# Low parts of weights and tokens moved from GpSimd to VectorE, PSUM banks split 3 and 5, and a new order of the MLPs' work

## The chip, the cores and the metric

The kernel runs on one core of a Trainium2 chip. The metric is device time in microseconds (us) of one execution, the median of three runs. One execution was also taken with the hardware profiler; all rows below are from that one.

## The reference

Attention with a threshold, then two MLPs on its output of 2304 tokens of 512 features. Everything is float32.

```python
def _attn_ref(q, k, v, tau):                      # 4 x 8 heads, 576 x 64
    scores = scale * np.matmul(q, k.transpose(0, 1, 3, 2))
    thresh = np.max(scores, axis=-1, keepdims=True) - tau
    scores = np.where(scores >= thresh, scores, -1000000000.0)
    ...
    return np.matmul(attn, v)
def _moe_ref(x, w_in, w_out):                     # 512 x 2048, 2048 x 512
    h = x @ w_in
    return (h * np.tanh(softplus(h))) @ w_out
def _moe2_ref(x, w_gate, w_val, w_out):           # 512 x 1536 twice, 1536 x 512
    g = x @ w_gate
    silu = g * (1.0 / (1.0 + np.exp(-g)))
    return (silu * (x @ w_val)) @ w_out
```

## The kernel before

Every product of the MLPs is three TensorE products: each operand is split into a high part, which ScalarE rounds, and a low part, the operand less its high part. The weights come as 64-bit words; VectorE and GpSimd take them apart and round them, and then split them.

The work is a list of steps. For each, the program gives an engine, an estimated cost, what must be done before, which buffers it takes and frees, and a rank. A planner (`Plan.run`) plays the list through with those costs: at each moment, among the steps whose estimated start lies within 0.06 us of the earliest, it takes the one with the lowest rank. What results is a fixed order of instructions on each engine. On the chip each engine works through its queue in that order, and an instruction that waits holds up all behind it.

The MLPs are cut into 140 units, numbered t from 0: 80 of the first MLP, 60 of the second. A unit is one block of 128 hidden features for one chunk of tokens; there are five chunks, four of 512 tokens and one of 256. The weights' blocks are worked off in groups (of 2, 2, 3, 3, 4, 2 blocks, then of 2, 3, 3, 2, 2); in a group, for each chunk, its blocks follow each other and add up in the same four PSUM banks, and then the sums leave PSUM. Unit numbers of the first groups: 0 to 9, 10 to 19, 20 to 34. The steps are called:

- U, of 12 matmuls: products with the first weights (`project`). In the second MLP U is the gate and a second one of 12 the value (called U2 in the code, V here with its unit, as V106). Each takes one bank of the pool `h`.
- E: Mish or Silu on ScalarE, which frees the bank of U. times: gate by value on VectorE, which frees the bank of V.
- H and O: the high part on ScalarE (line 541), the low part on VectorE (line 544).
- D0 to D139, of 12 matmuls: products with the last weights (`down`), in four quarters d, each into its own bank of the pool `y`. D of a unit needs its O.
- S: the eviction of a finished sum, four for a chunk, named by the last unit of the group on that chunk (S1,0 to S1,3 for chunk 0 of the first group). In an MLP's first group ScalarE copies it (line 572), later VectorE adds it to what is in SBUF (line 574). S frees its bank of `y`; D of the next chunk waits for that.
- w4 to w67: the weight tiles that are made beside the MLPs (w0 to w3 are made beside attention). For each: a load, then a, b (VectorE), u (GpSimd, line 443), c, d, e, x (VectorE; the last is line 457), h (ScalarE, line 462), and the low part (line 467, GpSimd).
- x and X, x2 and X2: high and low part of the tokens that an MLP reads, four pieces for each chunk (lines 548 and 551, ScalarE and GpSimd). The X of chunks 1 to 4 come at the start of the first MLP, the X2 of all five chunks at the change from the first to the second MLP.

The numbers of buffers and the ranks are in these lines (677 and 679):

```python
MSLOTS = dict(h=4, y=4, t=3, g=3, wraw=2, wc=2, wt=11)
MRANK = dict(X=-12.5, w=-17, U=1.5, U2=-13, D=21.5, E=-45, V=-28.5, H=-20, O=-17.5, S=19.5, x2=26.5, out=-40)
```

Of the kernel before, what the change touches and what calls it, by code (L numbers as in the profile page):

```python
# [20 lines left out]
def f(ap):  # L21
    return ap.bitcast(F32)
# [388 lines left out]
class Weights:  # L411
# [7 lines left out]

    def ops(self, plan, k, rank, place, t1, f1, t2, f2, after=()):  # L420

# [42 lines left out]
        def lo():  # L464
            m, j, _ = self.tiles[k]
            t = self.done[id(m), j]
            nc.gpsimd.tensor_tensor(out=t[:, 1], in0=f(self.n[k]), in1=f(t[:, 0]), op=ALU.subtract)  # L467

        K = lambda s: ("w", k, s)
        for eng, cost, fn, s, deps, take, free in (  # L470
            ("DMA", 1.46, load, "l", "", t1, []),
            ("DVE", .335, a, "a", "l", t2, []),
            ("DVE", .602, b, "b", "a", [], []),
            ("Pool", 1.0, up, "u", "b", [], []),
            ("DVE", .335, c, "c", "a", [], []),
            ("DVE", .335, d, "d", "u", [], []),
            ("DVE", .602, e, "e", "d", [], f1),
            ("DVE", .602, x, "x", "ec", [], []),
            ("ACT", .52, hi, "h", "x", [("wt", k)], []),
            ("Pool", 1.225, lo, "", "h", [], f2),  # L480
        ):
            plan.op(eng, cost, fn, K(s), [K(y) for y in deps] + list(after) * (s == "h"), take, free, rank - (20 if s == "l" else 0))


def moes(tc, cp, acc, W, uses, x0, units1, units2, w_in, w_out, w_gate, w_val, w_out2, out, chunk):
# [125 lines left out]
    for k in range(len(W.tiles)):  # L611
        if k < NEARLY:
            plan.given.add(("w", k, ""))
        else:
            W.ops(plan, k, when[uses[k]] + MRANK["w"], place, ["wraw"], ["wraw"], ["wc"], ["wc"])
    prev = {}
    for t, un in enumerate(units1 + units2):
# [33 lines left out]
        for d in range(width):  # L651
# [4 lines left out]
            if un["one"]:  # L656
# [131 lines left out]
```

## Time and profile before

| | us |
|---|---|
| median of three runs (lowest, highest) | 1183.14 (1181.34, 1183.83) |
| the profiled execution | 1182.31 |
| its span, first to last instruction | 1180.5 |
| TensorE busy in the span | 1125.4 |
| VectorE busy | 778.0 |
| ScalarE busy | 457.5 |
| GpSimd busy | 352.2 |

In the rows PE is TensorE, PEld its weight loads, DVE VectorE, ACT ScalarE, POOL GpSimd. Times in rows count from the span's start. Attention takes the first 314 us, the MLPs the rest. The 1.8 us between span and execution lie around the program.

### The profile page before, as it was taken

To read this page: it belongs to the slowest core of one execution; us is meant where nothing else is said; L and a number is where in the kernel's file an instruction comes from. 1 tells how busy PE (TensorE), PEld (TensorE's weight loads), DVE (VectorE), ACT (ScalarE), POOL (GpSimd) and SP (SyncE) were. 2 spreads that over 40 slices of the span, in tenths; PEclk is the share of its full clock that TensorE was granted. 3 is DMA by queue.
4 is the path that set the end of the run, shared out by engine and by line. 5 is a ranking of instruction groups with operands and counts; after the bars stand their busy time and mean duration, and the time that the engine had idled before them with its cause. 6 is when DMAs were issued, how large, how long until landed. Compare 5 with 4: busy or idle time off the path is not lost.

```text
span 1180.5 us, 16366 instructions
## 1 busy us (share of the span) xinstructions
PE 1125.4 (95%) x6088; PEld 928.3 (79%) x6088; DVE 778.0 (66%) x1291; ACT 457.5 (39%) x897; POOL 352.2 (30%) x452
## 2 busy tenths in 40 slices
PE   1899999999997999999999998999999999999998
PEld 1687777777686888888888876888888788888887
DVE  7888887888489883593753599627525873586333
ACT  3788787787644322232222233333111221121111
POOL 4555444443475330130210256502101320141000
PEclk9999999999999999999999999999999999999999
DMA  6465665664013211110120122101101120120012
GB/s 191 102 163 155 153 172 144 153 164 129 12 56 102 76 37 36 36 57 16 37 72 1 36 57 70 53 1 46 62 1 37 54 72 1 36 72 1 1 72 90
DMA packets 34272, 83.25 MB, mean 71 GB/s; under 512 B 5264, under 2 KB 5264, under 8 KB 34192
## 3 DMA queue, kind: packets, MB, share of 16 engines
q1 hardware_dynamic: 34192, 82.20, 24.6%
q8 instruction: 48, 0.79, 0.3%
q14 instruction: 32, 0.26, 0.1%
HBM read 50.92 MB, written 4.72 MB: 47 GB/s over the span
## 4 chain that ended last, share of the span: by engine, by line
PE 81%; DVE 11%; POOL 2%; DMA 2%; issue 2%; SPq 1%; ACT 1%; ACTq 0%; DVEq 0%; POOLq 0%
PE h L524 24%; PE y L535 13%; PE y L537 12%; PE v L524 12%; PE s L89 7%; PE av L172 6%; PE tg L149 6%; POOL xlo L551 2%; DVE gl L544 1%; DVE cg L453 1%; DVE cg L436 1%; DVE cn L457 1%; DVE cn L446 1%; DVE cg L439 1%; DVE cg L449 1%
## 5 line engine op out<-in xcount | busy, mean ns | idle before, releaser
L544 DVE TENSOR_TENSOR gl<-s,gh 128x512 fp32r<-128x512 f32 (+1 forms) x140 | 104.6, 748 | 122.9 <-ACT gh L541 122.8
L541 ACT CAST gh<-s 128x512 fp32r<-128x512 f32 (+1 forms) x140 | 81.0, 579 | 253.8 <-DVE s L565 111.4
L524 PE MATMUL h<-xhi,wt 128*128 128x512 f32 (+1 forms) x576 | 170.7, 363 | 0.0
L467 POOL TENSOR_TENSOR wt<-cn,wt 128x512 fp32r<-128x512 f32 x42 | 59.4, 1418 | 321.2 <-ACT wt L462 276.6
L89 PE MATMUL s<-stk 128*128 128x320 f32 (+5 forms) x672 | 126.0, 317 | 26.6 <-DVE pp L126 14.7
L565 DVE TENSOR_TENSOR s<-v,u 128x512 f32<-128x512 f32 (+1 forms) x60 | 38.1, 635 | 170.6 <-PE v L524 170.6
L535 PE MATMUL y<-gh,wt 128*128 128x512 f32 (+1 forms) x400 | 115.0, 372 | 10.8 <-DVE acc L574 9.2
L89 PEld LDWEIGHTS s<-stk 128*128 128x128 f32 (+1 forms) x672 | 98.1, 190 | 34.0 <-issue 19.9
L108 DVE TENSOR_REDUCE sm<-s 128x1 f32<-128x576 f32 x144 | 108.7, 755 | 24.0 <-PE s L89 23.8
L126 DVE SCALAR_TENSOR_TENSOR pp<-s,sm,e 128x576 f32<-128x576 f32 x144 | 116.0, 806 | 4.6 <-POOL sm L112 1.1
L524 PEld LDWEIGHTS h<-xhi,wt 128*128 128x128 f32 x576 | 104.8, 189 | 17.0
L118 ACT ACTIVATE e<-s,sm 128x576 f32<-128x576 f32 x144 | 109.3, 759 | 8.9 <-DVE sm L108 8.1
L149 PE MATMUL tg<-idf,pp 128*128 128x128 f32 x656 | 104.0, 284 | 3.6 <-DVE pp L126 2.3
L524 PE MATMUL h<-xlo,wt 128*128 128x512 f32 (+1 forms) x288 | 104.7, 363 | 0.0
L443 POOL TENSOR_TENSOR cg<-cg,ione 128x512 int32<-128x512 int32 x68 | 82.3, 1211 | 72.8 <-DVE cg L439 69.3
L155 ACT COPY pt<-tg 128x384 f32<-128x384 f32 x192 | 87.2, 493 | 32.1 <-PE tg L149 31.8
L524 PE MATMUL h<-xhi,early 128*128 128x512 f32 (+1 forms) x320 | 94.4, 362 | 0.0
L535 PEld LDWEIGHTS y<-gh,wt 128*128 128x128 f32 x400 | 73.2, 191 | 25.0 <-issue 8.4
L556 ACT ACTIVATE s<-h 128x512 f32<-128x512 f32 (+1 forms) x80 | 44.3, 555 | 121.6 <-PE h L524 117.9
L149 PEld LDWEIGHTS tg<-idf,pp 128*128 128x128 f32 x656 | 72.7, 142 | 23.6 <-ACT pt L155 5.0
L562 ACT ACTIVATE u<-h 128x512 f32<-128x512 f32 (+1 forms) x60 | 33.2, 554 | 141.1 <-PE h L524 141.1
L467 POOL TENSOR_TENSOR early<-cn,early 128x512 fp32r<-128x512 f32 x26 | 36.9, 1420 | 164.2 <-ACT early L462 129.8
(108 smaller groups left out, 2337.1 us busy)
## 6 DMA issues: line engine op xcount, KB each, us to landing
raw<-in_dram SPq DMA_DIRECT2D x64, 512.0 KB, 3.5
stk<-kh SPq DMA_DIRECT2D x60, 144.0 KB, 2.7
stk<-kl SPq DMA_DIRECT2D x60, 144.0 KB, 2.6
vn<-in_dram SPq DMA_DIRECT2D x16, 320.0 KB, 2.9
out_dram<-acc SPq DMA_DIRECT2D x18, 256.0 KB, 2.1
qn<-in_dram SPq DMA_DIRECT2D x15, 288.0 KB, 3.2
kn<-in_dram SPq DMA_DIRECT2D x15, 288.0 KB, 3.7
stk<-qh SPq DMA_DIRECT2D x30, 144.0 KB, 3.8
```

The costliest lines, as they stand in the source:

```text
L89: nc.tensor.matmul(out=s[out, c0:c0 + n], lhsT=stk[:, 0, qc:qc + out.stop - out.start], rhs=stk[:, w, kc:kc + n], start=w == 1, stop=w == 2)
L108: nc.vector.tensor_reduce(out=d["nm"][:, i:i + 1], in_=d["s", i], op=ALU.max, axis=AX.X, negate=True)
L118: nc.scalar.activation(out=e, in_=d["s", i], func=AF.Exp, bias=d["nm"][:, i:i + 1])
L126: nc.vector.scalar_tensor_tensor(out=d["pp", c][:, 576 * h:576 * h + 576], in0=d["s", i], scalar=d["th"][:, i:i + 1], in1=d["e", i], op0=A ...
L149: nc.tensor.transpose(g[:, 128 * m:128 * m + 128], d["pp", c][:, o:o + 128], idf)
L155: nc.scalar.copy(out=t[:, m0:m0 + n, 128 * (c % 2):128 * (c % 2) + 128], in_=g[:, 0:n])
L443: nc.gpsimd.tensor_tensor(out=g, in0=g, in1=self.ione.to_broadcast([P, 512]), op=ALU.add)
L467: nc.gpsimd.tensor_tensor(out=t[:, 1], in0=f(self.n[k]), in1=f(t[:, 0]), op=ALU.subtract)
L524: nc.tensor.matmul(out=un[nm], lhsT=w[:, a, P * d:P * d + P], rhs=parts(x, d, un["c0"], un["n"]), start=d == 0 and k == 0, stop=d == ND - ...
L535: nc.tensor.matmul(out=y[:, 0:un["n"]], lhsT=w[:, a, P * d:P * d + P], rhs=x, start=first and k == 0, stop=last and k == 2)
L537: nc.tensor.matmul(out=y, lhsT=x[:, P * d:P * d + P], rhs=w[:, a], start=first and k == 0, stop=last and k == 2)
L544: V.tensor_tensor(out=un["gl"], in0=un["s"], in1=f(un["gh"]), op=ALU.subtract)
```

## The change

Four things change, all in the MLPs.

1. The low part of the weights w4 to w67 (line 467 before) goes from GpSimd to VectorE. Those of w0 to w3, beside attention, stay on GpSimd.
2. The low part of the second MLP's tokens (X2) goes from GpSimd to VectorE. That of the first MLP's (X) stays.
3. `h` has three banks and `y` five.
4. The ranks are new, and each step of a weight has a rank of its own, where one rank served all ten. The planner's costs of some steps change too (GpSimd's steps and matmuls a little dearer).

```diff
-            nc.gpsimd.tensor_tensor(out=t[:, 1], in0=f(self.n[k]), in1=f(t[:, 0]), op=ALU.subtract)
+            (V if low == "DVE" else nc.gpsimd).tensor_tensor(out=t[:, 1], in0=f(self.n[k]), in1=f(t[:, 0]), op=ALU.subtract)
...
-            ("Pool", 1.225, lo, "", "h", [], f2),
+            (low, .602 if low == "DVE" else 1.4, lo, "", "h", [], f2),
...
-            plan.op(eng, cost, fn, K(s), [K(y) for y in deps] + list(after) * (s == "h"), take, free, rank - (20 if s == "l" else 0))
+            plan.op(eng, cost, fn, K(s), [K(y) for y in deps], take, free, rank[s])
...
-                    plan.op("Pool", po(n), lambda a=(d, c0, un["n"]): x_lo(*a), ("X2", c0, d), [("x2", c0, d)], [], [], r + MRANK["x2"])
+                    plan.op("DVE", dv(n), lambda a=(d, c0, un["n"]): x_lo(*a, V), ("X2", c0, d), [("x2", c0, d)], [], [], r + MRANK["x2"])
...
-MSLOTS = dict(h=4, y=4, t=3, g=3, wraw=2, wc=2, wt=11)
-
-MRANK = dict(X=-12.5, w=-17, U=1.5, U2=-13, D=21.5, E=-45, V=-28.5, H=-20, O=-17.5, S=19.5, x2=26.5, out=-40)
+MSLOTS = dict(h=3, y=5, t=3, g=3, wraw=2, wc=2, wt=11)
+
+MRANK = dict(X=319.9, wl=-583.5, ..., wh=2429.7, w=589.2, U=-76.1, U2=-833.8, D=-58.3, E=1768.7, V=-350.2, H=-1017.8, O=572.6, S=-939.1, x2=686.6, out=-1641.3)
...
-            W.ops(plan, n, EARLY[n], place, ["wraw"], ["wraw"], ["wc"], ["wc"])
+            W.ops(plan, n, {x: EARLY[n] - 20 * (x == "l") for x in ("l", "a", "b", "u", "c", "d", "e", "x", "h", "")}, place, ["wraw"], ["wraw"], ["wc"], ["wc"], "Pool")
```

TensorE's order in attention is the same as before; on GpSimd two neighbours there change places. The order of the MLPs is new throughout. Three places follow.

**The start of the MLPs.** VectorE's queue before, from the last piece of attention's output on (`acc` is that output, `cg` and `cn` a weight in the making, `gl` the result of O):

```order
L210 TENSOR_TENSOR acc_61<-av15_1_4111,rs15_1_4122 128x320
L436 TENSOR_SCALAR cg_4172<-raw_4171 128x512
L544 TENSOR_TENSOR gl_4201<-s_4190,gh_4200 128x512
L439 SCALAR_TENSOR_TENSOR cg_4172<-raw_4171,cg_4172 128x512
L446 TENSOR_SCALAR cn_4173<-raw_4171 128x512
L436 TENSOR_SCALAR cg_4187<-raw_4186 128x512
L439 SCALAR_TENSOR_TENSOR cg_4187<-raw_4186,cg_4187 128x512
L544 TENSOR_TENSOR gl_4229<-s_4216,gh_4228 128x512
```

The same place now, from the first step of a weight on:

```order
L437 TENSOR_SCALAR cg_4169<-raw_4168 128x512
L440 SCALAR_TENSOR_TENSOR cg_4169<-raw_4168,cg_4169 128x512
L447 TENSOR_SCALAR cn_4170<-raw_4168 128x512
L437 TENSOR_SCALAR cg_4187<-raw_4186 128x512
L440 SCALAR_TENSOR_TENSOR cg_4187<-raw_4186,cg_4187 128x512
L447 TENSOR_SCALAR cn_4188<-raw_4186 128x512
L450 TENSOR_SCALAR cg_4169<-cg_4169 128x512
L454 SCALAR_TENSOR_TENSOR cg_4169<-raw_4168,cg_4169 128x512
L450 TENSOR_SCALAR cg_4187<-cg_4187 128x512
L458 SCALAR_TENSOR_TENSOR cn_4170<-cn_4170,cg_4169 128x512
L454 SCALAR_TENSOR_TENSOR cg_4187<-raw_4186,cg_4187 128x512
L545 TENSOR_TENSOR gl_4243<-s_4229,gh_4242 128x512
```

O0 stood behind one step of a weight; now it stands behind eleven, five of them behind two steps u of GpSimd. GpSimd's queue has u of w4 and w5 after the first five X now, where they stood after all sixteen. On ScalarE, the queue at the same place, before (`xhi` is x, `s` the result of E, `gh` that of H):

```order
L548 CAST xhi_4153<-acc_61 128x512 x6
L556 ACT_TABLE_LOAD
L556 ACTIVATE s_4190<-h_4158 128x512
L548 CAST xhi_4153<-acc_61 128x512
L541 CAST gh_4200<-s_4190 128x512
L548 CAST xhi_4153<-acc_61 128x512 x2
L556 ACTIVATE s_4216<-h_4181 128x512
```

and now:

```order
L549 CAST xhi_4153<-acc_61 128x512 x12
L549 CAST xhi_4153<-acc_61 128x256 x4
L557 ACT_TABLE_LOAD
L557 ACTIVATE s_4229<-h_4158 128x512
L557 ACTIVATE s_4234<-h_4182 128x512
L542 CAST gh_4242<-s_4229 128x512
L542 CAST gh_4249<-s_4234 128x512
```

E0 stood after six of the sixteen x; now it stands after all of them.

**The first evictions of the second pair of chunks (S3), on ScalarE.** Before (`acc<-y` is S, `wt` the high part of a weight):

```order
L541 CAST gh_4386<-s_4352 128x512
L556 ACTIVATE s_4406<-h_4380 128x512
L572 COPY acc_61<-y_4347 128x512
L572 COPY acc_61<-y_4359 128x512
L572 COPY acc_61<-y_4366 128x512
L541 CAST gh_4431<-s_4406 128x512
L572 COPY acc_61<-y_4375 128x512
```

and now:

```order
L557 ACTIVATE s_4393<-h_4353 128x512
L463 CAST wt7_4396<-cn_4281 128x512
L542 CAST gh_4420<-s_4393 128x512
L557 ACTIVATE s_4445<-h_4415 128x512
L463 CAST wt8_4451<-cn_4360 128x512
L573 COPY acc_61<-y_4388 128x512
L573 COPY acc_61<-y_4398 128x512
L573 COPY acc_61<-y_4404 128x512
L542 CAST gh_4474<-s_4445 128x512
```

S3,0 stood behind E6; now the high part of w8 is between. Further down before, the high part of w8 stood between two pieces of S5.

**The end of the first MLP, on TensorE** (each `y` is one bank; `y_7499` and `y_7507` are the first of D78, the next chunk's sum, `h` is U). Before:

```order
L535 MATMUL y_7422<-gh_7303,wt31_6809 128x512 x2
L535 MATMUL y_7422<-gl_7304,wt31_6809 128x512
L535 MATMUL y_7427<-gh_7303,wt31_6809 128x512 x2
L535 MATMUL y_7427<-gl_7304,wt31_6809 128x512
L535 MATMUL y_7499<-gh_7364,wt30_6389 128x256 x2
L535 MATMUL y_7499<-gl_7365,wt30_6389 128x256
L535 MATMUL y_7507<-gh_7364,wt30_6389 128x256 x2
L535 MATMUL y_7507<-gl_7365,wt30_6389 128x256
```

and now:

```order
L536 MATMUL y_7423<-gh_7305,wt31_6805 128x512 x2
L536 MATMUL y_7423<-gl_7306,wt31_6805 128x512
L536 MATMUL y_7433<-gh_7305,wt31_6805 128x512 x2
L536 MATMUL y_7433<-gl_7306,wt31_6805 128x512
L525 MATMUL h_7464<-x0h_85,early2_83 128x512
L525 MATMUL h_7464<-x0l_86,early2_83 128x512
L525 MATMUL h_7464<-x0h_85,early2_83 128x512 x2
L525 MATMUL h_7464<-x0l_86,early2_83 128x512
```

D78 followed D77 at once; now U81 and V81, 24 matmuls, stand between. Where D35 and D50 open a new sum, a whole U stands ahead of each now; before, it was none and a quarter of one.

## Rows read from the trace of the kernel before

**Rows 1.** The page's first part: busy time and share of the span of each engine.

```profile
PE 1125.4 (95%) x6088; PEld 928.3 (79%) x6088; DVE 778.0 (66%) x1291; ACT 457.5 (39%) x897; POOL 352.2 (30%) x452
```

**Rows 2.** Stretches: length, each engine's busy us (instructions), granted clock, DMA.

```profile
core 0: us, PE busy (x) PEld busy (x) DVE busy (x) ACT busy (x) POOL busy (x), PEclk, DMA share, GB/s
355.00:400.00 45.00, 38.37 (x169) 30.89 (x168) 44.51 (x60) 17.62 (x37) 23.40 (x17) 0.96 0.28 89
...
700.00:745.00 45.00, 37.34 (x173) 31.19 (x172) 41.07 (x51) 16.63 (x30) 28.89 (x22) 0.92 0.20 59
...
679.00:742.00 63.00, 55.34 (x260) 46.34 (x259) 59.88 (x78) 23.66 (x43) 39.47 (x29) 0.95 0.23 67
```

**Rows 3.** Waits of TensorE: who for whom, us in total, times, longest.

```profile
PE y L535 <- DVE acc L574: 10.0, 4, 6.0
PE y L535 <- ACT acc L572: 6.6, 4, 3.2
...
PE y L537 <- ACT gh L541: 0.9, 1, 0.9
```

**Rows 4.** Timeline of TensorE at the two longest waits: start, us, [idle before].

```profile
363.19 1.22 PE L535 MATMUL y<-gh,early 128*128 128x512 f32 x2 [3.15 <-ACT acc L572]
...
364.63 1.05 PE L535 MATMUL y<-gh,early 128*128 128x512 f32 x2
...
738.16 0.77 PE L535 MATMUL y<-gh,wt 128*128 128x256 f32 x2 [5.99 <-DVE acc L574]
```

**Rows 5.** The chain that ended last: start, us, what; one undisturbed U.

```profile
403.95 2.72 PE h L524 x12
```

**Rows 6.** Timeline of ScalarE at the wait of 363 us.

```profile
362.03 0.62 ACT L462 CAST wt<-cn 128x512 fp32r<-128x512 f32 x1 [4.96 <-DVE cn L457]
362.56 0.58 ACT L572 COPY acc<-y 128x512 f32<-128x512 f32 x1
```

**Rows 7.** Timeline of VectorE, four steps of weights between 346 and 365 us.

```profile
346.09 0.42 DVE L446 TENSOR_SCALAR cn<-raw 128x512 int32<-128x512 int32 x1
...
360.14 1.26 DVE L446 TENSOR_SCALAR cn<-raw 128x512 int32<-128x512 int32 x1
361.32 0.68 DVE L457 SCALAR_TENSOR_TENSOR cn<-cn,cg 128x512 f32<-128x512 f32 x1
...
363.10 1.65 DVE L457 SCALAR_TENSOR_TENSOR cn<-cn,cg 128x512 f32<-128x512 f32 x1
```

**Rows 8.** Timeline of GpSimd at the same time.

```profile
359.69 1.42 POOL L443 TENSOR_TENSOR cg<-cg,ione 128x512 int32<-128x512 int32 x1 [1.90 <-DVE cg L439]
362.73 1.46 POOL L467 TENSOR_TENSOR wt<-cn,wt 128x512 fp32r<-128x512 f32 x1 [1.61 <-ACT wt L462]
```

**Rows 9.** Groups by line and shape, whole span: count, busy us, mean ns.

```profile
L443 POOL TENSOR_TENSOR cg<-cg,ione 128x512 int32<-128x512 int32 x68 | 82.3, 1211 | 72.8 <-DVE cg L439 69.3 <-PE y L535 2.4 <-PE y L537 1.1
...
L467 POOL TENSOR_TENSOR wt<-cn,wt 128x512 fp32r<-128x512 f32 x42 | 59.4, 1418 | 321.2 <-ACT wt L462 276.6 <-DVE cg L439 42.2 <-issue 2.1
```

**Rows 10.** Timeline at the start of the MLPs, TensorE, ScalarE, GpSimd, then VectorE.

```profile
314.68 0.50 PE L524 MATMUL h<-x0h,early 128*128 128x512 f32 x1 [0.67 <-DVE acc L210]
...
314.70 3.23 ACT L548 CAST xhi<-acc 128x512 fp32r<-128x512 f32 x6 [3.07 <-DVE acc L210]
317.94 1.28 ACT L556 ACT_TABLE_LOAD   x1
...
325.67 1.02 ACT L548 CAST xhi<-acc 128x256 fp32r<-128x256 f32 x3
...
315.40 21.59 POOL L551 TENSOR_TENSOR xlo<-acc,xhi 128x512 fp32r<-128x512 f32 x16 [8.21 <-ACT xhi L548]
...
320.90 1.37 DVE L544 TENSOR_TENSOR gl<-s,gh 128x512 fp32r<-128x512 f32 x1 [5.76 <-ACT gh L541]
...
331.62 4.08 DVE L544 TENSOR_TENSOR gl<-s,gh 128x512 fp32r<-128x512 f32 x3
...
338.03 1.25 DVE L449 TENSOR_SCALAR cg<-cg 128x512 int32<-128x512 int32 x1 [2.33 <-POOL cg L443]
```

More of the change, by code (lines that the diff above doesn't have):

```diff
@@ L418, in __init__, with ops @@
         self.raw, self.g, self.n, self.done = {}, {}, {}, {}
-    def ops(self, plan, k, rank, place, t1, f1, t2, f2, after=()):
+    def ops(self, plan, k, rank, place, t1, f1, t2, f2, low):
         nc, V = self.nc, self.nc.vector
@@ L473, in ops @@
             ("DVE", .602, b, "b", "a", [], []),
-            ("Pool", 1.0, up, "u", "b", [], []),
+            ("Pool", 1.1, up, "u", "b", [], []),
             ("DVE", .335, c, "c", "a", [], []),
@@ L548, in x_hi, with x_lo @@
         nc.scalar.copy(out=parts(0, d, c0, n), in_=acc1[:, d, c0:c0 + n])
-    def x_lo(d, c0, n):
-        nc.gpsimd.tensor_tensor(out=parts(1, d, c0, n), in0=acc1[:, d, c0:c0 + n], in1=f(parts(0, d, c0, n)), op=ALU.subtract)
+    def x_lo(d, c0, n, eng):
+        eng.tensor_tensor(out=parts(1, d, c0, n), in0=acc1[:, d, c0:c0 + n], in1=f(parts(0, d, c0, n)), op=ALU.subtract)
     def mish(un):
@@ L590, in moes @@
     for un in units1 + units2:
-        when.append(when[-1] + un["n"] * (.01 if un["one"] else .015))
+        when.append(when[-1] + un["n"] * (.0106 if un["one"] else .0159))
     aP, aS, aB = (lambda n, c=c: c + n / 1200 for c in (.05, .093, .187))
+    mm = lambda n: .04 + n / 800
     dv, po = (lambda n: .069 + n / 960), (lambda n: .04 + n / 418)
@@ L604, in moes @@
             plan.op("ACT", aS(n), lambda a=(d, c0, n): x_hi(*a), ("x", c0, d), [], [], [], r)
-            plan.op("Pool", po(n), lambda a=(d, c0, n): x_lo(*a), ("X", c0, d), [("x", c0, d)], [], [], r)
+            plan.op("Pool", po(n), lambda a=(d, c0, n): x_lo(*a, nc.gpsimd), ("X", c0, d), [("x", c0, d)], [], [], r)
     def place(k):
@@ L614, in moes @@
         else:
-            W.ops(plan, k, when[uses[k]] + MRANK["w"], place, ["wraw"], ["wraw"], ["wc"], ["wc"])
+            W.ops(plan, k, {x: when[uses[k]] + MRANK["w" + x] for x in ("l", "a", "b", "u", "c", "d", "e", "x", "h", "")}, place, ["wraw"], ["wraw"], ["wc"], ["wc"], "DVE")
     prev = {}
@@ L631, in moes @@
             for d in range(ND):
-                op("PE", n / 800, project, "h", w_in, d, key=("U", t, d), after=[K(w_in), ("X", c0, d)] + [("U", t, d - 1)] * (d > 0), take=["h"] * (d == 0), free=use(w_in, d == ND - 1))
+                op("PE", mm(n), project, "h", w_in, d, key=("U", t, d), after=[K(w_in), ("X", c0, d)] + [("U", t, d - 1)] * (d > 0), take=["h"] * (d == 0), free=use(w_in, d == ND - 1))
             op("ACT", aP(n), mish, key=("E", t), after=[("U", t, ND - 1)], take=["t"], free=["h"])
             made = ("E", t)
-            m, width, cost = w_out, ND, n / 800
+            m, width, cost = w_out, ND, mm(n)
         else:
             for d in range(ND):
-                op("PE", n / 800, project, "h", w_gate, d, key=("U", t, d), after=[K(w_gate), ("X2", c0, d)] + [("U", t, d - 1)] * (d > 0), take=["h"] * (d == 0), free=use(w_gate, d == ND - 1))
+                op("PE", mm(n), project, "h", w_gate, d, key=("U", t, d), after=[K(w_gate), ("X2", c0, d)] + [("U", t, d - 1)] * (d > 0), take=["h"] * (d == 0), free=use(w_gate, d == ND - 1))
             for d in range(ND):
-                op("PE", n / 800, project, "v", w_val, d, key=("U2", t, d), after=[K(w_val), ("U", t, ND - 1) if d == 0 else ("U2", t, d - 1)], take=["h"] * (d == 0), free=use(w_val, d == ND - 1))
+                op("PE", mm(n), project, "v", w_val, d, key=("U2", t, d), after=[K(w_val), ("U", t, ND - 1) if d == 0 else ("U2", t, d - 1)], take=["h"] * (d == 0), free=use(w_val, d == ND - 1))
             op("ACT", aP(n), silu, key=("E", t), after=[("U", t, ND - 1), ("E", n1 - 1)], take=["t"], free=["h"])
@@ L643, in moes @@
             made = ("V", t)
-            m, width, cost = w_out2, n // P, .64
+            m, width, cost = w_out2, n // P, mm(512)
         op("ACT", aS(n), hi, key=("H", t), after=[made], take=["g"])
@@ L676 @@
 MWAIT = 0.06
-MSLOTS = dict(h=4, y=4, t=3, g=3, wraw=2, wc=2, wt=11)
-MRANK = dict(X=-12.5, w=-17, U=1.5, U2=-13, D=21.5, E=-45, V=-28.5, H=-20, O=-17.5, S=19.5, x2=26.5, out=-40)
+MSLOTS = dict(h=3, y=5, t=3, g=3, wraw=2, wc=2, wt=11)
+MRANK = dict(X=319.9, wl=-583.5, wa=-1264, wb=369.6, wu=-2583.3, wc=593, wd=428.5, we=18.7, wx=272.7, wh=2429.7, w=589.2, U=-76.1, U2=-833.8, D=-58.3, E=1768.7, V=-350.2, H=-1017.8, O=572.6, S=-939.1, x2=686.6, out=-1641.3)
 @with_exitstack
```

## The prediction

> **What bounds the kernel now.** I read the page's shares first: TensorE is busy 1125.4 us of the span, VectorE 778.0 [rows 1]. In the MLPs TensorE runs at its pace, one U of 12 matmuls in 2.72 us, 0.227 each [rows 5], so only what it waits can be won there. The waits by name say for what: a bank of `y`, whose eviction is late on VectorE (10.0 us, four times) or on ScalarE (6.6, four times), and once an H (0.9) [rows 3]. That is 17.5 us. The stretches show where: from 355 to 400 us TensorE lacks 45 - 38.4 = 6.6 us while VectorE is busy 44.5 of 45, and from 700 to 745 us 7.7 while VectorE has 41.1 [rows 2]. The timeline shows a second loss behind the two longest waits: after 3.15 us of idling two matmuls take 1.05 us, so they start 0.43 apart, at the lower of the clock's two levels, 1.2 GHz; the granted clock of the stretch is 0.96 [rows 2, 4]. Seven matmuls stand there at that pace: 7 x 0.2 = 1.4 us. After the 5.99 us it is thirteen, nine of them half as wide: about 1.6. All that could be won after 314 us is thus 17.5 + 3.0 = 20.5 us: **8.0** (6.6 + 1.4) in the first stretch, **12.5** later.
>
> Why are evictions late? At 362.0 us ScalarE has stood 4.96 us before the high part of a weight, since VectorE had not made it, and the copy out of PSUM behind it came at 362.6 [rows 6]. VectorE itself is slowed by GpSimd: a step of 0.42 us takes 1.26 and ends just after GpSimd's u, one of 0.68 takes 1.65 and ends just after GpSimd's low part of a weight [rows 7, 8]. So a u costs VectorE some 0.85 us and a low part on GpSimd about 1.0. While GpSimd ran its sixteen X without a break (21.59 us, 1.35 each), VectorE got about one step done for each: ten from 320.90 to 335.70, 1.48 each [rows 10].
>
> **Part 1, low parts on VectorE.** An undisturbed long step takes 0.68 us, the next starts 0.60 on (two rows of rows 7 overlap by that). 64 weights: each adds 0.60 and removes about 1.0 of hindrance, where GpSimd's 1.42 us [rows 9] fell beside VectorE's work. The 20 X2 add 0.60 and remove between 0 and 1.1 each, since some met VectorE idle or at an addition from PSUM. In the stretch from 679 to 742 us, where both come together, seven weights and 15 X2 add 22 x 0.60 = 13.2 and remove 7.0 + (0 to 16.5): from +6 to -10 us on a VectorE that has 59.9 of 63 us [rows 2]. I take 0 there: not a relief, but no burden. The Trainium skill (SBUF — State Buffer, section "SBUF: two separate sides") says that VectorE and GpSimd lock their shared port pair for a whole instruction; the trace agrees (1.65 in place of 0.68), and by it u will still hinder.
>
> **Part 2, five banks and new order.** With four banks D78 waits for the first piece of S77, whose D77 stands directly ahead on TensorE. With five, the first quarter of D78 has a bank, and its second needs that piece, with U81 and V81 between: 24 x 0.227 = 5.4 us of cover. D35 and D50 get 2.7 us (one U); their waits were among the four of VectorE's 10.0 us. VectorE's lag grows over the stretch to its 59.9 us less what TensorE's products need, 55.3 busy less 1.6 of slow clock [rows 2], so to 6.2 us; of that 0.8 comes through 5.4 us of cover. At D74 the cover is one U and a quarter, 3.4 us, against half the lag. I leave **1.0** us (0 to 4). At D106 the order puts seven steps of weights ahead of the value's product and the low part O106 that D106 needs; added up they end about as late as D106 is due: **0.6** (0 to 1). So of 12.5 us 10.9 go. Three banks for `h` cost nothing there: a U needs the bank of three takes earlier, which is freed a whole U and D ahead.
>
> **Part 3, the start of the MLPs.** Here the new order adds waits that the trace does not have.
> - U3 is now the first to need a bank back, that of E0, and E0 stands behind all sixteen x. They start at 314.70: twelve at 0.525 (six took 3.23) and four at 0.31 are 7.5 us, the table load 1.28, E0 0.60 [rows 10]: 324.1, with its signal 324.3. TensorE, from 314.68 on, ends U2 at 323.0. **1.3** us (0.8 to 1.6).
> - O0 stands behind w4 d, e, w5 d, w4 x, w5 e, and these behind u of w4, which GpSimd starts after five X. Twelve long and four half as wide X took 21.59 us; with two thirds for a short one, a long one is 1.47. So u starts at 322.8 and ends at 323.9. In the trace d of w4 then took 1.25 us [rows 10], beside the second u: 325.1. Then X follows X on GpSimd again, six of them until 333.9, and VectorE does one step in 1.48: e, d, x, e, O0 end at 332.4, D0 can start at 332.6. TensorE has U3, half of U4 behind it at 324.3 + 4.1 = 328.4. **4.2** us. If GpSimd did not hinder, O0 would be there at 327.4: 0. I take the upper end, since rows 10 show this stretch with the same stream of X.
> - Such a wait is like the 3.15 us in rows 4, which the lower clock followed: **1.4** us (0 to 2.8).
> - D4's second quarter needs the first piece of S3, behind the high part of w8 on ScalarE. On VectorE 30 steps stand between O0 and w8's last: ten of 0.34, twenty of 0.60, 15.4 us; four u at 0.85, six X at 0.5 to 1.05 and a short wait for signals make it 23.3: 355.7. Cast and copy [rows 6] and signals: 357.3. TensorE comes there at 332.6 + 21.1 + 1.4 = 355.1. **2.2** us (0 to 5). Where the start costs less, this costs more: VectorE sets it.
> - By the same sum O9 is due about when D9 is: **0.5** us (0 to 1). The later S of the group stand clear of weights' casts.
>
> - u of w6 and w7 now stand ahead of the last five X. These end by 346; the first is due in U6, at about 349: nothing. SP issues the same loads in the same order.
>
> Together 9.6 us, against the 8.0 that the stretch loses now. Attention's two exchanged neighbours on GpSimd are nothing: the one thresh waits for a row maximum that comes after the low part's start, and no mask needs it sooner.
>
> **Sum.** 1182.3 (the profiled execution, 0.07% under the median) - 20.5 + 9.6 + 1.6 = **1173.0 us**, 0.8% under the time now.
>
> **Rivals.** (a) The start is mild: GpSimd lets VectorE through, O0 is in time and only U3 and some of D4 remain, 4.3 us; later nothing is left. 1182.3 - 20.5 + 4.3 = 1166. For it: some steps in rows 7 are not hindered. Against: the 1.48 a step in rows 10. (b) Gains are given back: the start at its upper ends, 14.5 us, and 5 us later on: 1181.3. For it: VectorE is full in both stretches. (c) **Slower.** VectorE becomes the bound between the MLPs: the 13.2 us moved onto it come on top of its 59.9 and the hindrance is not from the low parts but from u and X2's neighbours, so nothing is removed. Then it needs 73.1 us where products need 53.7, and TensorE loses 19.4 there in place of 1.0: 1191. It decides, that is the kernel gets slower than now, once under 6 us of hindrance are removed. Against it stand 1.65 and 0.68 in rows 7. The Trainium skill (Perfetto Trace Analysis, section "Optimizing Scalar/DVE Operations") speaks for (c), as it would take work off a saturated VectorE, even to GpSimd, and against it, as the shared port may undo that; no run here shows yet which. (d) That the change does not do what it says is excluded: the orders show both moves.
>
> **How the numbers follow.** Forecast, 1167 to 1179: 0.62. (a): 0.16. (b): 0.14, two thirds of it still under the time now by over 0.2%. (c): 0.08, some of it near no change. What a measurement can tell from no change is about 0.2%, 2.4 us: faster means under 1180.8. Faster 0.62 + 0.16 + 0.09 = 0.87, same 0.07, slower 0.06. The range takes in (a), the forecast and most of (b), 1165 to 1181.
>
> **What would show it.** Right: in the profile after, TensorE waits for E at U3 (1.3 us), for O0 at D0 (3 to 5 us, behind X on GpSimd), for S3 at D4; the six-microsecond wait at D78 is gone; steps of 1.65 us on VectorE beside low parts are gone; 0.68 for the new low parts; GpSimd falls by some 60 x 1.4 and 20 x 1.5 us. Wrong: O0 in time at D0; a VectorE over 60 us in the stretch between the MLPs with TensorE waiting for S or X2; a wait of over 1 us in the second half of the second MLP, where I see none.

## The result, and the profile after

The changed kernel takes **1168.83 us** (median of 4 runs, 1168.42 to 1170.29) against 1182.66 before in the same comparison: ratio 0.9886, 95% interval 0.9868 to 0.9903. That is 13.8 us, where the prediction had 9.3 against its profiled execution. The profiled execution after took 1168.52 us, its span is 1166.7.

In the profile after, the lines moved: `project` is L525, `down` L536 (first MLP) and L538, E L557, H L542, O L545, S L573 (ScalarE) and L575 (VectorE), a weight's steps a, b, u, c, d, e, x, h, low are L437, L440, L444, L447, L450, L454, L458, L463, L468; x is L549, X and X2 L552.

The page's busy line, answering [rows 1]:

```profile
PE 1122.5 (96%) x6088; PEld 928.0 (80%) x6088; DVE 757.0 (65%) x1375; ACT 457.8 (39%) x897; POOL 246.1 (21%) x368
```

VectorE has 84 instructions more (64 weights, 20 X2) and is busy 21.0 us less. The stretches of [rows 2], columns as there:

```profile
core 0: us, PE busy (x) PEld busy (x) DVE busy (x) ACT busy (x) POOL busy (x), PEclk, DMA share, GB/s
355.00:400.00 45.00, 43.41 (x214) 36.55 (x214) 40.13 (x69) 20.60 (x42) 11.54 (x8) 1.00 0.33 105
700.00:745.00 45.00, 45.00 (x222) 38.23 (x221) 43.64 (x80) 19.30 (x37) 7.42 (x5) 1.00 0.23 70
679.00:742.00 63.00, 63.00 (x302) 53.12 (x301) 59.77 (x110) 26.35 (x49) 13.65 (x9) 1.00 0.22 68
```

Between the MLPs TensorE is busy 63.00 of 63 us. VectorE is as busy there as before, 59.77, but it now serves TensorE's full pace (302 matmuls in place of 260; the order has also moved some of VectorE's steps out of this stretch or into it). The waits of TensorE in the MLPs, answering [rows 3] (for whom, us, times, longest):

```profile
PE y L536 <- DVE gl L545: 4.5, 1, 4.5
...
PE y L536 <- ACT acc L573: 1.6, 1, 1.6
PE h L525 <- ACT s L557: 1.1, 1, 1.1
```

All the waits for VectorE's additions (10.0 us before) are gone. The three that stand are those at D0, D4 and U3; the timeline of TensorE has them, and a fourth small one at D106 (start, us, [idle before]):

```profile
324.07 0.50 PE L525 MATMUL h<-xhi,early 128*128 128x512 f32 x1 [1.11 <-ACT s L557]
...
328.30 0.61 PE L536 MATMUL y<-gh,early 128*128 128x512 f32 x2
333.38 0.80 PE L536 MATMUL y<-gl,early 128*128 128x512 f32 x1 [4.47 <-DVE gl L545]
333.97 1.05 PE L536 MATMUL y<-gh,early 128*128 128x512 f32 x2
...
357.94 0.73 PE L536 MATMUL y<-gh,early 128*128 128x512 f32 x2 [1.59 <-ACT acc L573]
...
918.47 0.50 PE L538 MATMUL y<-wt,gl 128*128 128x512 f32 x1 [0.32 <-DVE gl L545]
```

Behind D0's wait two matmuls take 1.05 us, as in [rows 4]: eleven matmuls stand 0.43 apart, at the lower level of the clock, 1.2 GHz. The stretch with it (columns as above):

```profile
328.00:338.00 10.00, 5.53 (x16) 4.08 (x15) 10.00 (x11) 2.15 (x4) 6.46 (x5) 0.66 0.31 102
```

### The profile page after: what moved, and what is told of

It reads as the page before. It is cut to its first block, busy times and chain, and to the rows that moved or that the text cites. A ratio compares the mean times of both kernels' runs of the same rounds, so it can differ in the third digit from the quotient of the medians.

```text
span 1166.7 us, 16261 instructions
## 1 busy us (share of the span) xinstructions
PE 1122.5 (96%) x6088; PEld 928.0 (80%) x6088; DVE 757.0 (65%) x1375; ACT 457.8 (39%) x897; POOL 246.1 (21%) x368
## 4 chain that ended last, share of the span: by engine, by line
PE 91%; DVE 5%; POOL 2%; issue 1%; ACT 0%; SPq 0%; DMA 0%; ACTq 0%; DVEq 0%
PE h L525 27%; PE y L536 16%; PE v L525 12%; PE y L538 12%; PE s L89 8%; PE tg L149 7%; PE av L172 7%; DVE cg L454 1%; DVE cn L458 1%; PE rg L197 1%; POOL xlo L552 1%; DVE gl L545 1%; DVE cg L450 1%; POOL cg L444 0%; SPq L76 0%
## 5 line engine op out<-in xcount | busy, mean ns | idle before, releaser
L444 POOL TENSOR_TENSOR cg<-cg,ione 128x512 int32<-128x512 int32 x68 | 92.2, 1360 | 627.9 <-DVE cg L440 627.9
L542 ACT CAST gh<-s 128x512 fp32r<-128x512 f32 (+1 forms) x140 | 80.9, 579 | 257.3 <-DVE s L566 126.4
L525 PE MATMUL h<-xhi,wt 128*128 128x512 f32 (+1 forms) x576 | 170.5, 363 | 0.0
L545 DVE TENSOR_TENSOR gl<-s,gh 128x512 fp32r<-128x512 f32 (+1 forms) x140 | 98.9, 708 | 107.6 <-ACT gh L542 106.3
L89 PE MATMUL s<-stk 128*128 128x320 f32 (+5 forms) x672 | 126.2, 317 | 26.1 <-DVE pp L126 14.2
L108 DVE TENSOR_REDUCE sm<-s 128x1 f32<-128x576 f32 x144 | 108.6, 754 | 24.6 <-PE s L89 24.4
L525 PEld LDWEIGHTS h<-xhi,wt 128*128 128x128 f32 x576 | 104.7, 189 | 17.3
L536 PE MATMUL y<-gh,wt 128*128 128x512 f32 (+1 forms) x400 | 113.3, 368 | 0.0
L525 PE MATMUL h<-xlo,wt 128*128 128x512 f32 (+1 forms) x288 | 104.5, 363 | 0.0
L525 PE MATMUL h<-xhi,early 128*128 128x512 f32 (+1 forms) x320 | 95.0, 363 | 1.1 <-ACT s L557 1.1
L557 ACT ACTIVATE s<-h 128x512 f32<-128x512 f32 (+1 forms) x80 | 44.2, 555 | 124.6 <-PE h L525 121.8
L172 PE MATMUL av<-pt,vn 128*64 128x256 f32 (+1 forms) x640 | 84.7, 411 | 0.0
L536 PEld LDWEIGHTS y<-gh,wt 128*128 128x128 f32 x400 | 72.6, 189 | 12.5
L575 DVE TENSOR_TENSOR acc<-y,acc 128x512 f32<-128x512 f32 (+1 forms) x100 | 60.6, 633 | 29.7 <-PE y L536 29.7
```

The lines of the kernel that those rows point to most:

```text
L89: nc.tensor.matmul(out=s[out, c0:c0 + n], lhsT=stk[:, 0, qc:qc + out.stop - out.start], rhs=stk[:, w, kc:kc + n], start=w == 1, stop=w == 2)
L108: nc.vector.tensor_reduce(out=d["nm"][:, i:i + 1], in_=d["s", i], op=ALU.max, axis=AX.X, negate=True)
L172: nc.tensor.matmul(out=d["av", u][64 * h:64 * h + 64, 0:n], lhsT=d["vn"][:, 5 * h + j], rhs=d["pt", u][:, 5 * h + j if j < 4 else 4, 0:n], ...
L444: nc.gpsimd.tensor_tensor(out=g, in0=g, in1=self.ione.to_broadcast([P, 512]), op=ALU.add)
L525: nc.tensor.matmul(out=un[nm], lhsT=w[:, a, P * d:P * d + P], rhs=parts(x, d, un["c0"], un["n"]), start=d == 0 and k == 0, stop=d == ND - ...
L536: nc.tensor.matmul(out=y[:, 0:un["n"]], lhsT=w[:, a, P * d:P * d + P], rhs=x, start=first and k == 0, stop=last and k == 2)
```

## The experiments

To compare stretches, I took for each kernel the intervals from start to start of the MLPs' matmuls, less the pace (0.227 us, half that for 256 columns), and subtracted the same sum in the best kernel found (e7 below), in which TensorE waits for nothing in the MLPs. What is left is what TensorE loses. The MLPs' length is from the first to the last matmul's start; e7's is 837.4 us (314.76 to 1152.11).

| kernel | median us | MLPs, us | lost to 400 us | 400 to 700 | 700 to 745 | after 745 | sum |
|---|---|---|---|---|---|---|---|
| before | 1182.5 | 861.7 | 9.7 | 2.8 | 9.9 | 2.0 | 24.4 |
| both moves alone (e5) | 1172.05 | 851.7 | 6.1 | 2.2 | 4.6 | 1.5 | 14.4 |
| order and banks alone (e10) | 1180.01 | 859.6 | 14.2 | -0.1 | 5.9 | 2.3 | 22.2 |
| changed kernel | 1168.83 | 848.1 | 10.1 | -0.1 | 0.1 | 0.6 | 10.7 |
| changed, with spare GpSimd work (e9) | 1182.79 | 861.4 | 16.2 | 1.5 | 3.0 | 3.4 | 24.1 |
| true prices, low parts on GpSimd (e12) | 1164.94 | 844.3 | 0.0 | 0.3 | 4.3 | 2.3 | 6.9 |
| true prices (e7) | 1158.53 | 837.4 | 0 | 0 | 0 | 0 | 0 |

(Before: median of the 19 runs beside e9 and e10. "True prices": the planner is given longer times for VectorE's steps, see e7 below.)

### The moves, taken back one by one (e1, e2)

The changed kernel and its order; e1 has the weights' low parts on GpSimd again, e2 the X2.

```diff
-            (V if low == "DVE" else nc.gpsimd).tensor_tensor(out=t[:, 1], in0=f(self.n[k]), in1=f(t[:, 0]), op=ALU.subtract)
+            nc.gpsimd.tensor_tensor(out=t[:, 1], in0=f(self.n[k]), in1=f(t[:, 0]), op=ALU.subtract)
```

```diff
-  ... lambda a=(d, c0, un["n"]): x_lo(*a, V), ("X2", c0, d) ...
+  ... lambda a=(d, c0, un["n"]): x_lo(*a, nc.gpsimd), ("X2", c0, d) ...
```

> The changed kernel with one thing undone: the low parts of weights w4 to w67 run on GpSimd again. Every engine's order is that of the changed kernel, only these 64 instructions stand in GpSimd's queue at their place. Theory (the new order, with its cover at chunk openings, brings the gain; the engine of the low parts matters little): VectorE saves 0.60 us and loses about 1.0 of hindrance for each, so D4's wait grows by four times 0.4, 1.6 us, and the openings later on stay covered: 1171 to 1173 us. Rival (the gain is the hindrance that left VectorE): waits for S return at D35, D50, D74 and D78, 1177 us or more.

> The changed kernel with one thing undone: the 20 low parts of the second MLP's tokens (X2) run on GpSimd again, all orders else kept. Theory: the stretch between the MLPs has cover, 0 to 2 us more: 1169 to 1171. Rival (hindrance): the wait at D78 comes back by 3 to 6 us: 1172 to 1175.

e1: **1176.82 us** (1175.92 to 1177.64), 8.0 over the changed kernel. e2: **1171.27** (1171.21 to 1171.93), 2.4 over it. The theory that I held, the moves are load-neutral, falls with e1: taken back, the weights' low parts alone cost 8.0 of the 13.8 us. The rival met the time, but not the places: waits for additions came back to 1.1 us only, while D4's grew from 1.6 to 3.8 and D106's from 0.3 to 1.2. e2 fell between its two ranges. Two reserves. Of what e2 loses, summed as in the table, 1.5 us lie before 400 us, where its edit changes nothing, and 1.5 between 700 and 745 us, where the X2 are; so the X2 are not shown to be worth more than 1.5. And in e1's profiled execution the MLPs are 5.8 us longer than after (853.9 against 848.1), and another 2.2 us lie ahead of them, in attention, which the edit does not touch; the execution's first matmul came 1.2 us later. Why is open.

### The banks alone (e3, e4)

e3 is the changed kernel with four and four banks, e4 the kernel before, its order kept, with three and five.

```diff
-    ph, py = pool("ph", B["h"], space=PSUM), pool("py", B["y"], space=PSUM)
+    ph, py = pool("ph", 4, space=PSUM), pool("py", 4, space=PSUM)
```

```diff
-    ph, py = pool("ph", B["h"], space=PSUM), pool("py", B["y"], space=PSUM)
+    ph, py = pool("ph", 3, space=PSUM), pool("py", 5, space=PSUM)
```

> The changed kernel with the order kept to the instruction, but four banks in each of the two PSUM pools. Theory (banks act through the order that they let the planner make): an opening waits for the piece of S that it would have met a quarter later, 0.7 us more at D4, nothing where a U stands between: 1169.5 to 1170.5. Rival (the fifth bank itself takes the waits away): 6 us more, about 1175, with waits at every opening.

> The kernel before with its order kept to the instruction, but three banks for products and five for sums. Theory: each of the eight waits at openings is shortened by one quarter of D, 0.68 us (0.36 for 256 tokens), some 4 us in all: 1178 to 1181. Rival (the fifth bank itself): 10 us less, 1173 or under.

e3: **1170.28** (1169.49 to 1171.42), 1.4 over the changed kernel, which is not clear of noise: the intervals of the two ratios to before overlap (0.9883 to 0.9913 and 0.9868 to 0.9903), and in the profile the MLPs are only 0.7 us longer (848.8 against 848.1). The theory's 0.7 us more at D4 did not come: that wait is 1.7 us in place of 1.6. With four banks for U, instead, the wait at U3 is gone and the one at D0 is 5.8 in place of 4.5. e4: **1180.16** (1179.09 to 1181.97), 2.2 under before, ratio 0.9981 [0.9971, 0.9990]. In e4 the wait at D78 stands, one quarter later: 6.54 us from start to start at its second quarter, where before it was 6.38 at its first. A bank without cover between moves a wait; it does not take it away.

### The moves alone, and the order with banks alone (e5, e10)

e5 is the kernel before with its order and banks, and the two moves; e10 is the changed kernel with both moves taken back (the two edits of e1 and e2).

```diff
-            nc.gpsimd.tensor_tensor(out=t[:, 1], in0=f(self.n[k]), in1=f(t[:, 0]), op=ALU.subtract)
+            (V if k >= NEARLY else nc.gpsimd).tensor_tensor(out=t[:, 1], in0=f(self.n[k]), in1=f(t[:, 0]), op=ALU.subtract)
...
-  ... lambda a=(d, c0, un["n"]): x_lo(*a), ("X2", c0, d) ...
+  ... lambda a=(d, c0, un["n"]): x_lo(*a, V), ("X2", c0, d) ...
```

> The kernel before with its own order and its four and four banks; only the low parts of w4 to w67 and of X2 go to VectorE, at the places where GpSimd's stood. The orders of TensorE, ScalarE and the loads stay. Taking the two moves back out of the changed kernel cost 8.0 and 2.4 us. Theory A, they act by themselves, since GpSimd no longer hinders VectorE: 1182.3 - 10 = 1172, up to 1174, and in the trace the waits at D6 and D8 fall under 1 us each and that at D78 under 2. Theory B, they act only with an order that leaves cover: D78 still follows D77 at once and waits for the addition S77 (1 to 2 us), w8's high part still stands among the evictions of the first stretch: 3 to 6 us less, 1176 to 1179. Rival from the prediction, VectorE gets more to do in a stretch where it is full: no gain or a loss, 1182 to 1191.

> The changed kernel, its order and banks, with both low parts (w4 to w67 and X2) back on GpSimd. It is the fourth corner of: engine as before or changed, order and banks as before or changed. If the parts add up: 1168.8 + 8.0 + 2.4 = 1179.2 (1178 to 1181), and order with banks alone is worth some 3 us, the engine alone 10. Rival, order and banks already cover what GpSimd disturbs between the MLPs, so that the second move adds nothing: 1177; or they make each other worse, over 1182.

e5: **1172.05** (1171.22 to 1172.65), ratio 0.9902 [0.9888, 0.9917]. e10: **1180.01** (1179.28 to 1180.26), ratio 0.9981 [0.9971, 0.9990]. Against the table's 1182.5 the moves alone thus bring 10.4 us (11.0 against the 1183.07 measured beside e5), order and banks alone 2.5, both together 13.7: nearly the sum. Theory A holds in its time; single waits stayed longer than it said. e5's waits:

```profile
PE y L535 <- ACT acc L572: 4.5, 4, 1.6
PE y L535 <- DVE acc L574: 4.0, 3, 2.4
```

Against [rows 3] the additions fell from 10.0 to 4.0, and D78's from 6.0 to 2.4, with no change in order. In e10 it is the other way round: the wait at D78 is gone, through the order's 24 matmuls between, and the one at D74, the last of these rows, is the longest between the MLPs:

```profile
PE y L536 <- DVE gl L545: 4.4, 1, 4.4
PE y L536 <- ACT acc L573: 3.7, 1, 3.7
...
PE y L536 <- DVE acc L575: 2.7, 1, 2.7
```

### GpSimd work that nobody needs (e9)

The changed kernel, and behind each low part of w4 to w67 on VectorE one more instruction on GpSimd, of the form of the old low part, into a buffer that nobody reads.

```diff
             (V if low == "DVE" else nc.gpsimd).tensor_tensor(out=t[:, 1], in0=f(self.n[k]), in1=f(t[:, 0]), op=ALU.subtract)
+            if low == "DVE":
+                nc.gpsimd.tensor_tensor(out=self.spare, in0=f(t[:, 0]), in1=f(t[:, 0]), op=ALU.subtract)
...
+    W.spare = pa.tile([P, 512], F32R, name="spare")
```

> The changed kernel with its order, and on GpSimd, behind each low part of w4 to w67 that VectorE makes, one more instruction of the old one's form and size (128x512, some 1.42 us) that writes into a buffer that nobody reads; nothing waits for it but what follows it on GpSimd. Theory, a GpSimd instruction takes VectorE's time while it runs, whatever it is for: about 0.9 us for each of 60; the stretches where VectorE is full (to 400 us, 679 to 742) get longer, and TensorE waits there again: 1176 to 1186, that is at least what moving the low parts back cost (8.0 us), since VectorE keeps its own low parts. Rival, the 8.0 us came from the low part itself being ready 0.8 us later on GpSimd: 1168 to 1170.

**1182.79 us** (1181.79 to 1185.54), ratio to before 1.0005 [0.9996, 1.0015]: 64 instructions for which no other engine's step waits cost 14.0 us, the whole gain. The rival (the low part comes later from GpSimd) cannot be the cause here, since VectorE makes the low parts. Nor is it u, which now stands behind the spare work in GpSimd's queue: VectorE is idle before d, which waits for u, 15.7 us in sum, against 16.2 in the changed kernel. The page's busy line, then GpSimd and VectorE beside each other (the spare work is L470, the low part L468):

```profile
PE 1126.0 (95%) x6088; PEld 928.7 (79%) x6088; DVE 802.1 (68%) x1375; ACT 456.9 (39%) x897; POOL 339.3 (29%) x432
```

```profile
361.43 1.38 POOL L470 TENSOR_TENSOR spare<-wt 128x512 fp32r<-128x512 f32 x1 [1.95 <-ACT wt L463]
...
366.49 1.22 POOL L470 TENSOR_TENSOR spare<-wt 128x512 fp32r<-128x512 f32 x1
```

```profile
361.84 1.52 DVE L468 TENSOR_TENSOR wt<-cn,wt 128x512 fp32r<-128x512 f32 x1
363.28 0.68 DVE L458 SCALAR_TENSOR_TENSOR cn<-cn,cg 128x512 f32<-128x512 f32 x1
...
366.73 1.52 DVE L468 TENSOR_TENSOR wt<-cn,wt 128x512 fp32r<-128x512 f32 x1
```

VectorE's same 1375 instructions are busy 802.1 us in place of 757.0: 45.1 us, 0.70 for each spare instruction. Beside one a low part takes 1.52 us, the step after it 0.68. The Trainium skill (SBUF — State Buffer, section "SBUF: two separate sides") says that the shared port pair is locked for a whole instruction and the other engine blocks; the trace agrees.

### The start (e6, e8, e7, e11, e12)

e6 is the changed kernel, planned anew with E, H and O of the first three units ahead of all else. e8 keeps the ranks and tells the planner what VectorE's steps cost beside GpSimd. e7 has both. e11 is e7's order with four and four banks, e12 e7's order with both low parts on GpSimd (the edits of e1 and e2).

```diff
-            plan.op(eng, cost, lambda: fn(un, *a), key, after, take, free, r + MRANK[key[0]])
+            plan.op(eng, cost, lambda: fn(un, *a), key, after, take, free, -9999 if key[0] in "EHO" and key[1] < 3 else r + MRANK[key[0]])
```

```diff
+            if low == "DVE" and eng == "DVE":
+                cost = 1.3 if k < 8 else cost + .6 * (s == "c")
             plan.op(eng, cost, fn, K(s), [K(y) for y in deps], take, free, rank[s])
```

> The changed kernel, planned anew with E, H and O of the first three units ahead of everything else: E0 behind six of the x on ScalarE, O0 second on VectorE from the MLPs' start on. In the changed kernel TensorE loses 1.3 us at U3, 4.6 at D0 and 2.2 at the lower clock behind it. Theory, VectorE sets the start: these 8 us go at their places, but VectorE now stands some 4 us before O0 (H0 comes at about 321) and is slowed by X as long as before, so O2, the weights' steps and w8's high part come later and TensorE waits at D2 to D9 in their place: 1166 to 1170. Rival, the waits at the start come of the order alone and cover what follows: all 8 us go, 1160 to 1162.

e6: **1172.53** (1171.03 to 1173.48), 3.7 over the changed kernel. U3 and D0 wait no more, but:

```profile
PE y L536 <- ACT acc L573: 5.2, 1, 5.2
PE h L525 <- POOL xlo L552: 3.3, 2, 3.0
```

Both ranges are missed. The theory has it that waits come back later, but not their size: they came back larger than those that went. TensorE is at D4 earlier, but w8's high part comes to ScalarE at 357.5 us (356.8 in the changed kernel), and S3 still stands behind it; at U6 TensorE waits for an X that GpSimd's queue has behind u of w7. Both waits were followed by matmuls 0.43 apart.

> The prices of the run before in the changed kernel, but E, H and O of the first units keep their ranks: E0 stands behind all sixteen x, so U3 waits 1.3 us as in the changed kernel; O0 stands behind four steps of weights in place of eleven, but H0 comes at about 325.5 us, O0 at about 327: in time for D0, which is due at 328.4. Theory (D0's 4.6 us were the steps of weights under X ahead of O0): D0 waits under 1 us, no lower clock, S3 ahead of w8's high part takes the wait at D4: 1168.8 - 8 = 1160 to 1163, about as the run before. Rival (VectorE full): 1166 to 1170.

e8: **1159.94** (1159.82 to 1160.70). U3 waits its 1.11 us, D0 not at all. On VectorE two O stand directly behind four steps of weights (start, us, [idle before]), and end before D0 needs them:

```profile
315.96 2.40 DVE L440 SCALAR_TENSOR_TENSOR cg<-raw,cg 128x512 int32<-128x512 int32 x2
325.79 2.96 DVE L547 TENSOR_TENSOR gl<-s,gh 128x512 fp32r<-128x512 f32 x2 [7.43 <-ACT gh L544]
```

> As the run before, and the planner is told what the trace shows of VectorE: 1.3 us for a step of w4 to w7 (they lie beside X on GpSimd), and 0.6 more for step c later (beside u). It now puts O2, O3 and the evictions S1 and S3 ahead of the high parts of w4 to w8. Theory, TensorE waited in the first stretch because steps stood in the queues ahead of evictions which the planner's cheap prices had made look early: the waits at U3, D0, D4 go and little comes back: 1158 to 1163. Rival, VectorE is full until D9 whatever the order and a U of the second group then waits for w4 or w5: 1166 to 1171.

e7: **1158.53** (1158.01 to 1158.96), ratio to before 0.9790 [0.9774, 0.9806]: 10.3 us under the changed kernel, the best version found. The prices alone brought 8.9 of them (e8), the rank for the first units 1.4 more; without the prices that rank made the kernel slower (e6). TensorE waits nowhere in the MLPs but for their first operand (0.7 us), and its busy share is 97%:

```profile
PE 1119.6 (97%) x6088; PEld 926.9 (80%) x6088; DVE 751.2 (65%) x1375; ACT 460.3 (40%) x897; POOL 243.8 (21%) x368
```

VectorE is as busy as in the changed kernel (751.2 against 757.0). What changed is what stands ahead of what: the planner had counted a step beside X at 0.34 to 0.60 us, and the trace has 1.5 to 1.75; the 1.3 that it was given is still short of that.

> The kernel that was planned anew with VectorE's true prices and the rank for the first units (1158.5 us, no wait of TensorE left in the MLPs), its order kept, with four banks for products and four for sums. Theory, five banks are worth something only where an eviction is late, and here none is but that at the end of the first MLP: 1158.5 to 1160. Rival, the fifth bank carries the order: 1162 or more.

e11: **1158.45** (1158.18 to 1159.36). The fifth bank is worth nothing where evictions are early.

> The order that was planned with VectorE's true prices (1158.5 us, no wait of TensorE in the MLPs), kept as it is, with both low parts (w4 to w67 and X2) back on GpSimd. In the changed kernel's order the same step back cost 11 us. Theory, the order only moves where VectorE's lateness is felt and the load must go too: TensorE waits for S and the low parts O again, above all between the MLPs: 1163 to 1170. Rival, an order with the evictions early covers GpSimd's hindrance as well: 1158 to 1160, and the engine would not have mattered.

e12: **1164.94** (1163.19 to 1165.23), 6.4 over e7. Even in the best order the low parts on GpSimd cost; the longest wait stands between the MLPs, at D82:

```profile
PE y L540 <- ACT acc L582: 2.7, 1, 2.7
```

## Why the prediction was right, and where not

**The size of what could be won, wrong.** The prediction took 20.5 us: the waits by name, 17.5, and 3.0 of slow clock. By e7's MLPs it was 24.4. This is 3.9 of the 4.5 us between forecast and profiled execution. The idle time of a row counts from the modelled end of the matmul before, 0.39 us after its start, while the next would start after 0.227; each wait is thus 0.16 too short. D6's 3.15 of [rows 4] is 3.54 from start to start, so 3.31 lost. Summed in this way the nine waits that make up the 17.5 are 19.0 us, 1.5 more. The slow matmuls come to some 3.6, 0.6 more. The rest, near 1.8, lies in the first matmuls after each wait, 0.33 apart in place of 0.227, in a tenth wait that the 17.5 left out (0.5 us, for O at 932 us), and in what I did not separate.

**Part 1, "I take 0 there: not a relief, but no burden": near for VectorE's load, wrong for the time.** This is the step that failed in kind. The prediction's sum gives the moves nothing and so puts its whole gain, 9.3 us, down to order and banks. Alone, these bring 2.5 us (e10). The moves bring 10.4 us without the new order (e5) and 11.2 with it (e10 against the changed kernel).

VectorE's load in the stretch was sized well enough. Over the same matmuls, those from 679 to 742 us in the kernel before and then those from 679 to 742 us in the changed kernel, the rows are (before, e5; e10, changed kernel; columns as in [rows 2]):

```profile
679.11:742.08 62.97, 55.31 (x260) 46.31 (x258) 59.77 (x78) 23.55 (x43) 39.55 (x29) 0.95 0.23 67
673.55:731.94 58.39, 55.16 (x259) 45.88 (x258) 58.00 (x100) 24.03 (x43) 10.69 (x7) 0.97 0.23 73
683.49:752.19 68.70, 66.04 (x302) 55.29 (x300) 62.06 (x82) 25.89 (x48) 48.44 (x33) 0.95 0.20 62
679.16:742.10 62.94, 62.94 (x301) 53.07 (x300) 59.71 (x110) 26.45 (x49) 13.49 (x9) 1.00 0.22 68
```

With the order kept, the moves take 1.8 and 2.4 us off VectorE's busy time, inside the bounds of +6 to -10 and not far from 0. The same matmuls take 4.6 and 5.8 us less, though: the rest is time in which VectorE stood idle, 3.2 us before and 0.4 in e5, 6.6 in e10 and 3.2 now. In e10 4.6 of these are waits for GpSimd itself (for u, and for a buffer that a low part frees), now 3.1. What the other idle time comes from is not separated. The price of 1.0 us of hindrance for a low part was near: from 314 us on VectorE is busy 529.0 us in e10 and 504.5 in the changed kernel, with 84 instructions more of 0.68, so (24.5 + 57.1)/84 = 0.97 were removed for each. In the old order it is 0.83 (525.6 before, 512.8 in e5).

**Part 2, the residue right, the credit wrong.** D78, D35, D50 and D74 wait for nothing; the prediction left 1.0. D106 lost 0.5 where 0.6 stood. But the 10.9 us that it gave to banks and order are theirs only in part. In e10 they take the loss behind 400 us from 14.7 to 8.1 us, and add 4.5 in the first stretch; banks alone are worth 2.2 (e4) in the old order and 1.4, not clear of noise, in the new (e3). That the residue came out near is in part luck: the moves, which by the prediction bring nothing, took away the same waits.

**Part 3, the start, right.** 9.6 us were forecast; 9.9 can be read off: U3 1.3 for 1.3 (1.50 us from start to start), D0 4.6 for 4.2, the clock 2.2 for 1.4, D4 1.75 for 2.2, D9 nothing for 0.5. The chain that led to it stands in the trace as worked out. ScalarE:

```profile
314.52 7.58 ACT L549 CAST xhi<-acc 128x512 fp32r<-128x512 f32 x16 [3.07 <-DVE acc L210]
322.12 1.28 ACT L557 ACT_TABLE_LOAD   x1
323.42 1.08 ACT L557 ACTIVATE s<-h 128x512 f32<-128x512 f32 x2
...
356.78 0.62 ACT L463 CAST wt<-cn 128x512 fp32r<-128x512 f32 x1 [5.74 <-DVE cn L458]
357.31 1.55 ACT L573 COPY acc<-y 128x512 f32<-128x512 f32 x3
```

GpSimd:

```profile
315.23 7.66 POOL L552 TENSOR_TENSOR xlo<-acc,xhi 128x512 fp32r<-128x512 f32 x5 [8.21 <-ACT xhi L549]
322.85 2.02 POOL L444 TENSOR_TENSOR cg<-cg,ione 128x512 int32<-128x512 int32 x2
324.84 9.62 POOL L552 TENSOR_TENSOR xlo<-acc,xhi 128x512 fp32r<-128x512 f32 x6
```

VectorE:

```profile
323.91 1.25 DVE L450 TENSOR_SCALAR cg<-cg 128x512 int32<-128x512 int32 x1 [2.19 <-POOL cg L444]
325.20 1.67 DVE L454 SCALAR_TENSOR_TENSOR cg<-raw,cg 128x512 int32<-128x512 int32 x1
326.79 1.51 DVE L450 TENSOR_SCALAR cg<-cg 128x512 int32<-128x512 int32 x1
328.22 1.76 DVE L458 SCALAR_TENSOR_TENSOR cn<-cn,cg 128x512 f32<-128x512 f32 x1
329.90 1.75 DVE L454 SCALAR_TENSOR_TENSOR cg<-raw,cg 128x512 int32<-128x512 int32 x1
331.58 1.74 DVE L545 TENSOR_TENSOR gl<-s,gh 128x512 fp32r<-128x512 f32 x1
```

u starts at 322.85 (322.8 forecast); d, e, d, x, e and O0 take a step for each X, 1.6 us each where 1.48 stood, and O0 ends at 333.3 (332.4). w8's cast starts at 356.8, S3 behind it. To take the upper end of D0's range by [rows 10] was right. Read together, part 3 is off by 0.3 us, and parts 2 and 3 by 0.5: the forecast left 11.2 us of loss, the trace has 10.7.

**The rivals.** (a), 1166, was the nearest in time, but not in its mechanism: the start was not mild. (b) is out. (c), VectorE becomes the bound, is out by e5 and turned round by e9: it is GpSimd's work that makes VectorE full. The Trainium skill (Perfetto Trace Analysis, section "Optimizing Scalar/DVE Operations") suggests taking work off a saturated VectorE, even to GpSimd, and warns that the shared port may undo it. Here the warning decides: VectorE at 95% of its stretch [rows 2] gained by taking work back from GpSimd.

## What to carry to other kernels

Price a GpSimd instruction by what it takes from VectorE while it runs, not only by its own time; where VectorE is full, a step of 0.68 us on it can be cheaper than one of 1.4 us on GpSimd beside it. To say what is to be won on an engine that sets the pace, sum the intervals from start to start against the undisturbed pace, not the idle time in the rows. And where a planner sets the order, give it the durations that the trace shows in that stretch: that was worth 8.9 us on top of the change (e8), and 10.3 with the first units ranked ahead as well (e7), with the same instructions. And do not read the time saved from an engine's busy sum: 1.8 us less of it on VectorE went with 4.6 us less for TensorE.

## What the runs showed of the hardware

- Additions that read one operand from PSUM and one from SBUF are not slowed by GpSimd: a 128x512 S of the first MLP took 686 ns before, 687 after, 685 in e9 with the spare work. They did meet it: in the kernel before 22 of the first MLP's 100 additions overlap a GpSimd instruction, and the longest takes 692 ns. The steps that read only SBUF went meanwhile from 0.42 to 1.5 or from 0.68 to 1.75 us.
- Beside a stream of X on GpSimd VectorE does about one step for each instruction of GpSimd, short or long: a of 0.43 us alone took 1.52. GpSimd pays as well: the first five X took 7.66 us in the changed kernel beside a working VectorE, and 6.32 in e6, where VectorE waited for H0.
- After waits of 4.47 us (the changed kernel's D0) and 3.05 (e6's U6) matmuls came 0.43 apart, 1.2 GHz; after those of 1.59 and 1.11 us they did not. The length of the wait alone does not decide: of two waits of 2.42 us, the one at e5's D78 was followed by the lower level (granted clock 0.51 from 728 to 731 us), the one at 363 us in e4 was not (1.00 from 363 to 370), and one of 2.03 us at e2's D4 was (0.62 from 358 to 362.5). In e6 six intervals of 0.23 to 0.34 us came first, at D0 none.
